# Sparse attention into a softplus MLP on one core: whole-tile loads for the ramp, a V load moved between queues, and two more limits in the kernel's own planner

## The chip, the cores and the metric

The kernel runs on one core of one Trainium2 chip. Its time is the device time of one execution in microseconds (us), and the time of a kernel is the median over several runs. Engines are named as in the profile: PE is TensorE, DVE is VectorE, ACT is ScalarE, POOL is GpSimd, SP is SyncE. A name with a q (SPq, ACTq) is the queue of that engine from which DMAs are issued.

## The reference

Attention over B = 4 batches, H = 8 heads, S = 768 positions, D = 64 with a selection of key chunks, and then an MLP over the 3072 tokens. Cut to what matters:

```python
# attention: chunks of 32 keys, each query keeps the 6 chunks with the highest upper bound
k_min = min over each chunk of k;  k_max = max over each chunk of k
ub = sum over d of maximum(q * k_min, q * k_max)
ub = where(causal by chunk, ub, -1e9)
sel = the top 6 chunks of ub
scores = where(sel and pos_q >= pos_k, q @ k.T / sqrt(D), -1e9)
attn = softmax(scores) @ v
# MLP: tokens x 512 -> 2048 -> 512
h = x @ w_in
g = maximum(h, 0) + log1p(exp(-abs(h)))      # softplus
out = g @ w_out
```

## The kernel before

The work is cut into 12 blocks: 4 batches times 3 query blocks of 256 positions (QB = 256), each of two token tiles of 128 (NT = 2). Heads are taken in four pairs (NP = 4). For each block the kernel loads K, Q and V; brings K and Q into transposed form; reduces K to the minimum and maximum of each chunk (`kx`); forms positive and negative parts of Q (`qp`, `qn`, line 568); multiplies them with the chunk bounds on PE (`ub`, lines 588 and 589); adds the causal mask (L595), takes the largest eight per head (`max`, L604) and compares every chunk with the sixth (`lt`: a compare at L612 and a cast of one column per head at L615, for each token tile in each half of the heads). The comparison result is the mask `mr`. Transposed, it becomes extra rows of the score operands `qa` and `qb`, so that one score matmul (`s`, L691) adds the mask. Exponentials (L700) follow on ACT, the causal select on the diagonal (`cm`, L706) on POOL, the product with V (`av`, L716) on PE, the normalisation (L725, L737) on DVE. The MLP of a block is `h` (L773), exp and log (L779, L783: softplus as log(1 + exp)), and `y` (L794), then a copy (L799) and a store (L803).

The first three blocks (NRAMP = 3, called the ramp here) are prepared with transposes on PE from float32 (`kT` at L490, `qT` at L549, `mT` at L636), with copies on ACT and DVE. Blocks 3 to 11 are prepared with casts on POOL (L457, L459) and transposing DMAs on SP (L509, L559, L651 for the mask, L753 for the attention output).

No order is written by hand. `build` makes a graph of tasks, each with an engine, an assumed duration, a priority and the buffers that it reads and writes. `Graph.schedule` then plays the graph through in assumed time, engine by engine, and the order in which tasks were started becomes the order of the instructions in each engine's program. Some details matter here:

- A task marked `port=True` (and every POOL task that isn't a DMA) starts only when the other engine of DVE and POOL is not in such a task.
- Each DMA is put into a modelled queue after its issue; `lat` is added when it leaves the queue.
- While a spare PSUM buffer is kept (until WARM = 30 us of assumed time), PE gets a fill wherever it has nothing to do: a matmul on a tile of zeros (L355). The fills stand in the program and run whether or not PE would have had to wait.
- A few tasks have an alternative engine (`alt`): the mask copies `ma`, `mb` (L641), the copy `xe` (L750) and the V casts of the ramp (`vc`, L662) go to whichever engine takes them first.

`ramp_loads` issues the loads of the ramp. Of block 0, K and Q are loaded as four half tiles each, by SP and ACT in turn (L389); its two V tiles go one to SP and one to ACT (L386). For blocks 1 and 2, buffer `t` takes the columns of four heads of both token tiles, with two DMAs of 128 KB for each buffer. `hold_pool` (L415) makes POOL read one loaded tile before it issues the weights (L406 and L409, on POOL's queue); which tile, HOLD says. `hold_sp` (L421) does the same on SP for the loads of block 3 onward. In the program that is built, hardware DMAs (those of SP and ACT) take eight semaphores in turn, so each waits until the eighth before it has landed.

Of the kernel before, what the change touches and what calls it, by code (L numbers as in the profile page):

```python
# [13 lines left out]
ACT = mybir.ActivationFunctionType  # L14
# [19 lines left out]
OHP = -98.5  # L34
# [4 lines left out]
RLEAD = 3  # L39
# [7 lines left out]
HOLD = ("q", 0)  # L47
# [22 lines left out]
class Graph:  # L70
# [39 lines left out]
    def schedule(self):  # L110
# [6 lines left out]
        queues, moved = {}, 0.0  # L117
# [24 lines left out]
        def fits(t, eng):  # L142
            if t.alts[eng][2] and port["POOL" if eng == "DVE" else "DVE"] > now + 1e-9:
                return False
# [34 lines left out]
        while True:  # L179
# [27 lines left out]
            for e in LAT:  # L207
# [44 lines left out]
                if t.dma is None:  # L252
                    t.end = now + t.dur + t.lat
                    done(t, t.end)
                else:
                    post(now + DMA_START, "queue", t)
# [4 lines left out]
def build(nc, tiles):  # L261
# [115 lines left out]

    def ramp_loads(n, base, gate):
        for nm in "kqv":
            for t in range(2):  # L380
                b_ = XF[nm, n, t] = Buf("xf")

                def ld(eng, us, nm=nm, t=t, b_=b_):
                    dst = T(b_).rearrange("s (h d) -> s h d", d=D)
                    if nm == "v":
                        eng().dma_start(out=dst, in_=rows(nm, n, t))  # L386
                    else:
                        for u in us:
                            eng().dma_start(out=dst[:, u * 4:u * 4 + 4], in_=rows(nm, n, u)[:, t * 4:t * 4 + 4])  # L389
                pr = base + "kqv".index(nm) + 0.1 * t  # L390
                if n == 0 and nm != "v":
                    for u, eng in ((0, "SP"), (1, "ACT")):
                        add(eng, 0.6, lambda u=u, ld=ld: ld(lambda: AC if u else SP, [u]), pr, w=[(b_, u)],
                            dma=0.585, lat=0.5, name=f"ld{nm}{n}{t}", after=gate)
                else:
                    eng = "ACT" if n == 0 and t == 1 else "SP"
                    add(eng, 0.6 if nm == "v" else 1.2,
                        lambda eng=eng, ld=ld: ld(lambda: AC if eng == "ACT" else SP, range(NT)), pr,
                        w=[(b_, 0), (b_, 1)], dma=1.17, lat=0.5, name=f"ld{nm}{n}{t}", after=gate)

# [65 lines left out]
    def prep(n):  # L466
# [12 lines left out]
        if ramp:  # L479
            for hh in range(2):  # L480
                xk = XF["k", n, hh]
# [3 lines left out]
                def tr(xk=xk, kT=kT):  # L485
                    xv = T(xk).rearrange("s (t p c) -> s t p c", t=NT, p=2)
                    for p in range(2):
                        for t in range(NT):
                            c0 = (p * NT + t) * 128
                            PE.transpose(T(kT)[:, c0:c0 + 128], xv[:, t, p], T("identf"))  # L490
                add("PE", 0.44, tr, pr + 0.01 * hh, r=[(xk, 0), (xk, 1), "identf"], w=[kT], name=f"kT{n}")
# [437 lines left out]
```

## Time and profile before

| what | value |
|---|---|
| median of 8 runs | 265.6 us (264.99 to 267.08) |
| the profiled execution's own time | 264.99 us |
| its span, first to last instruction | 263.3 us |
| granted TensorE clock | 0.999 |
| PE busy | 255.5 us (97%), 2593 matmuls, 133 of them fills |
| ACT busy | 205.0 us (78%) |
| DVE busy | 146.4 us (56%) |
| POOL busy | 85.2 us (32%) |
| load of a K tile of 256 KB, issue to landing | 3.7 us median |
| transposing DMA of the mask, issue to landing | 3.8 us median |

A row of the groups gives line, engine, operation, output and inputs, count, then busy time and mean duration of one, then the engine's idle time before them and what ended it. A row of the timeline starts with the start and the length in us. A row of the chain of waits has start, length and what it was. Rows of PE overlap, since matmuls are pipelined: four matmuls of L773 start 0.109 us apart, though each row lasts 0.27. For DMAs the trace also has the time of each landing.

### The profile page before, as it was taken

Reading aid. Unit: us, or ns where it says so; the run is one execution under the profiler, and the core shown is the slowest. Engines: PE = TensorE matmul, PEld = TensorE weight load, DVE = VectorE, ACT = ScalarE, POOL = GpSimd, SP = SyncE. Lnnn points to the kernel's source line nnn. Section 1 sums busy time; section 2 is a strip of 40 time slices with the busy share of each in tenths; the row PEclk is TensorE's granted clock in tenths of the full one; section 3 lists DMA queues with packets and bytes.
Section 4 is the critical chain, followed back from the end, with each engine's and each line's share of the span. In section 5 each row is a group of like instructions: output and inputs, shape, how many; then the busy total and the mean of one; then the engine's idle time right before and its main releaser. Section 6 shows DMA issues by size and latency. Waiting matters only on the chain.

```text
span 263.3 us, 6800 instructions
## 1 busy us (share of the span) xinstructions
PE 255.5 (97%) x2593; PEld 192.4 (73%) x2593; DVE 146.4 (56%) x549; ACT 205.0 (78%) x369; POOL 85.2 (32%) x179
## 2 busy tenths in 40 slices
PE   8899999999998999999989999999999999999993
PEld 6789997677685776778668768768678778676751
DVE  7489784228597798559998549068363110210202
ACT  5588999997496968999569987949869789576650
POOL 5037542263254560637256521433211111100000
PEclk9999999999999999999999999999999999999999
DMA  7998999979996997999999955885112111130112
GB/s 183 254 223 154 206 206 204 239 98 260 173 268 100 221 244 169 260 225 241 151 232 197 267 139 131 193 167 82 41 46 78 40 41 42 40 84 0 42 40 80
DMA packets 121029, 39.90 MB, mean 152 GB/s; under 512 B 113668, under 2 KB 117764, under 8 KB 120996
## 3 DMA queue, kind: packets, MB, share of 16 engines
q1 hardware_dynamic: 113396, 33.83, 60.3%
q0 software_dynamic: 4448, 4.85, 10.8%
q10 hardware_dynamic: 3152, 0.79, 1.4%
q8 instruction: 20, 0.33, 0.5%
q14 instruction: 13, 0.11, 0.1%
HBM read 27.26 MB, written 6.29 MB: 127 GB/s over the span
## 4 chain that ended last, share of the span: by engine, by line
PE 80%; DVE 8%; DMA 5%; ACT 4%; issue 1%; ACTq 0%; DVEq 0%
PE ps L773 27%; PE ps L794 27%; PE ps L691 13%; PE ps L716 7%; PE ps L355 4%; DMA w<-in_q_dram 2%; DVE kx L513 2%; ACT pt L700 2%; DMA w<-mr 1%; DVE mr L615 1%; DMA w<-in_k_dram 1%; DVE ub L604 1%; ACT e L779 1%; PE ps L549 1%; PE ps L490 1%
## 5 line engine op out<-in xcount | busy, mean ns | idle before, releaser
L794 PE MATMUL ps<-w_out_sb,g 128*128 128x512 bf16 x384 | 106.6, 379 | 0.0
L773 PE MATMUL ps<-x,w_in_sb 128*128 128x256 bf16 x768 | 106.3, 272 | 0.0
L700 ACT ACTIVATE pt<-ps 128x512 bf16<-128x512 f32 (+1 forms) x192 | 93.5, 581 | 5.6 <-PE ps L691 5.3
L773 PEld LDWEIGHTS <-w_in_sb 128*128 128x128 bf16 x768 | 72.9, 98 | 24.8
L779 ACT ACTIVATE e<-ps 128x512 f32<-128x512 f32 x96 | 57.8, 628 | 35.2 <-PE ps L773 34.8
L706 POOL TENSOR_SCALAR_AFFINE_SELECT pt<-pt 128x256 bf16<-128x256 bf16 x96 | 41.0, 432 | 110.9 <-ACT pt L700 110.2
L783 ACT ACTIVATE g<-e 128x1024 bf16<-128x1024 f32 x48 | 51.8, 1080 | 0.9
L794 PEld LDWEIGHTS <-g 128*128 128x128 bf16 x384 | 35.0, 98 | 13.9 <-ACT g L783 0.4
L799 DVE COPY yo<-ps 128x512 f32<-128x512 f32 x24 | 16.4, 685 | 47.8 <-PE ps L794 47.8
L725 DVE RECIPROCAL st<-ps 128x4 f32<-128x4 f32 x48 | 8.6, 182 | 42.3 <-PE ps L716 32.8
L691 PE MATMUL ps<-qab,kb 128*128 128x256 bf16 x192 | 30.5, 259 | 0.2 <-ACT pt L700 0.2
L716 PEld LDWEIGHTS <-pt 128*128 128x128 bf16 x672 | 26.6, 97 | 4.3
L691 PE MATMUL ps<-qab,ka 96*128 96x256 bf16 x192 | 28.9, 259 | 0.9 <-DVE qab L654 0.9
L716 PE MATMUL ps<-v,pt 128*128 128x65 bf16 x672 | 28.5, 193 | 0.0
L459 POOL CAST w<-w 128x512 bf16<-128x512 f32 x36 | 22.0, 629 | 11.0 <-DMA w<-in_k_dram 10.1
L691 PEld LDWEIGHTS <-ka 96*128 96x128 bf16 x192 | 17.8, 97 | 8.5 <-issue 1.2
L513 DVE TENSOR_REDUCE kx<-w 128x32 bf16<-128x1024 bf16 x18 | 21.4, 1209 | 3.3 <-DMA w<-w 3.2
L355 PE MATMUL ps<-zero 128*128 128x256 bf16 x133 | 20.3, 297 | 1.1 <-DVE zero L325 1.1
L691 PEld LDWEIGHTS <-kb 128*128 128x128 bf16 x192 | 16.4, 97 | 6.1 <-issue 0.5
L355 PEld LDWEIGHTS <-zero 128*128 128x128 bf16 x133 | 13.7, 106 | 3.4 <-DVE zero L325 1.1
L737 DVE TENSOR_TENSOR w<-ps,st 128x256 bf16<-128x256 f32 x36 | 15.1, 421 | 1.1
L457 POOL CAST v<-w 128x512 bf16<-128x512 f32 x18 | 11.0, 622 | 12.2 <-DMA w<-in_v_dram 12.2
(64 smaller groups left out, 181.4 us busy)
## 6 DMA issues: line engine op xcount, KB each, us to landing
out_dram<-yo SPq DMA_DIRECT2D x24, 256.0 KB, 2.9
w<-in_v_dram SPq DMA_DIRECT2D x23, 256.0 KB, 3.8
w<-in_k_dram SPq DMA_DIRECT2D x18, 256.0 KB, 3.7
w<-in_q_dram SPq DMA_DIRECT2D x18, 256.0 KB, 4.2
w_in_sb<-in_moe_w_in_dram POOLq DMA_DIRECT2D x4, 512.0 KB, 8.7
w_out_sb<-in_moe_w_out_dram POOLq DMA_DIRECT2D x4, 512.0 KB, 15.1
w<-in_k_dram SPq DMA_DIRECT2D x10, 128.0 KB, 4.5
w<-in_q_dram SPq DMA_DIRECT2D x10, 128.0 KB, 3.8
```

The costliest lines, as they stand in the source:

```text
L355: PE.matmul(T(Fill)[:, 0:256], T("zero")[:, 0:128], T("zero"), start=True, stop=True)
L459: PO.tensor_copy(T(b_)[:, :, t], T(xf).rearrange("s (p c) -> s p c", p=NP))
L513: DV.tensor_reduce(T(kx)[:, m].rearrange("d p (t c) -> d p t c", t=NT), T(kt).rearrange("d (p t) (c s) -> d p t c s", t=NT, s=CH), axis=AX ...
L691: PE.matmul(T(sp)[:, z * QB:z * QB + QB - q0], kk[r0:r1, p, (j + z) * 128:(j + z + 1) * 128], qq[r0:r1, p, q0:QB], start=True, stop=True)
L700: AC.activation(T(pt)[:, j:j + 2].rearrange("k j c -> k (j c)")[:, 0:w], T(sp)[:, 0:w], ACT.Exp, scale=SCALE)
L706: PO.affine_select(out=diag, in_=diag, compare_op=ALU.is_ge, fill=0.0, base=0, channel_multiplier=-1, pattern=[[0, 2], [1, 128]])
L716: PE.matmul(o[:, u, h], T(pts[h])[:, j, c0:c0 + 128], T("v", i)[:, j, 2 * p + h, :], start=(j == 0), stop=(j == t0 + u))
L773: PE.matmul(o, T("w_in")[:, dt, ft * 128:(ft + 1) * 128], T(x)[:, dt], start=(dt == 0), stop=(dt == KDM - 1))
L779: AC.activation(T(e)[:, f2 * 2:f2 * 2 + 2].rearrange("f a s -> f (a s)"), T(hp), ACT.Exp)
L783: AC.activation(T(gb)[:, f4 * 4:(f4 + 1) * 4], T(e), ACT.Ln, bias=1.0)
L794: PE.matmul(T(y), T(gb)[:, f, u * 128:(u + 1) * 128], T("w_out")[:, f, :], start=(f == 0), stop=(f == KFF - 1))
L799: add("DVE", 0.6, lambda y=y, yo=yo: DV.tensor_copy(T(yo), T(y)), pr, r=[y], w=[yo], name=f"yo{n}")
```

## The change

In words, by the parts of the diff:

- Blocks 1 and 2 load K and Q as whole token tiles, one DMA of 256 KB for each, as V always did. `columns` and `landing` are new helpers: the transposes of the ramp take the columns of a head pair from the right buffer, and for blocks 1 and 2 each transpose group reads both token tiles.
- The second V tile of block 0 is issued from SP, as all V tiles are.
- `fits` refuses a DMA of SP or ACT while the eighth before it has not landed in the planner's time.
- The mask compare `lt` is marked as a user of the port that DVE and POOL share.
- Transposing DMAs get a landing latency of TLAT = 1.4 instead of 0.8.
- The constants: RLEAD from 3 to 1 (how far the preparation of a ramp block is put ahead of its attention), OHP from -98.5 to -96 (priority of the two ACT copies at L349), HOLD from `("q", 0)` to `("k", 0)` (the tile of block 2 that POOL waits for before the weights).

The planner places everything anew, so the order of the later blocks changes as well. The new program has 129 fills instead of 133 and the same other matmuls. SP issues 18 DMAs for the ramp instead of 25; ACT loses one DMA issue. One `ma` and one `mb` go from ACT to DVE, one `xe` from DVE to ACT; of the V casts of the ramp, ACT has one of block 0 and one of block 2 (before: one of block 0, one of block 1), POOL the other four.

```diff
 NEG = -30000.0 / SCALE
 BIG = 1.0e30
 NRAMP = 3
-OHP = -98.5
+OHP = -96.0
 W2 = 18
 WARM = 30.0
 COLD = 4.2
 TD = 1.9
-RLEAD = 3
+TLAT = 1.4
+RLEAD = 1
 OPRIO = 25.0
 LEAD = 22
 BG = 40
...
 MSTART = 14.0
 AHEAD = 1.16
 ORDER = "b0 b1 b2 i0 i1 i2 i3 o0 o1 o2 o3".split()
-HOLD = ("q", 0)
+HOLD = ("k", 0)
 
 
 LAT = {"PE": 0.23, "ACT": 0.20, "DVE": 0.15, "POOL": 0.15, "SP": 0.0}
...
         waiting = {e: [] for e in LAT}
         ready = {e: [] for e in LAT}
         events, seq, order = [], 0, []
-        queues, moved = {}, 0.0
+        queues, moved, flying = {}, 0.0, []
 
         def post(at, what, x):
             nonlocal seq
...
         port = {"DVE": 0.0, "POOL": 0.0}
 
         def fits(t, eng):
+            if t.dma is not None and eng != "POOL" and len(flying) >= 8 and (flying[-8].end is None or flying[-8].end > now):
+                return False
             if t.alts[eng][2] and port["POOL" if eng == "DVE" else "DVE"] > now + 1e-9:
                 return False
             for b in t.bufs:
...
                     t.end = now + t.dur + t.lat
                     done(t, t.end)
                 else:
+                    if e != "POOL":
+                        flying.append(t)
                     post(now + DMA_START, "queue", t)
         assert len(order) == len(self.tasks) + len(self.fills), (len(order), len(self.tasks))
         return order
...
     XF, KQ = {}, {}
     landed = {}
 
+
     def ramp_loads(n, base, gate):
         for nm in "kqv":
             for t in range(2):
                 b_ = XF[nm, n, t] = Buf("xf")
-
-                def ld(eng, us, nm=nm, t=t, b_=b_):
-                    dst = T(b_).rearrange("s (h d) -> s h d", d=D)
-                    if nm == "v":
-                        eng().dma_start(out=dst, in_=rows(nm, n, t))
-                    else:
-                        for u in us:
-                            eng().dma_start(out=dst[:, u * 4:u * 4 + 4], in_=rows(nm, n, u)[:, t * 4:t * 4 + 4])
                 pr = base + "kqv".index(nm) + 0.1 * t
                 if n == 0 and nm != "v":
                     for u, eng in ((0, "SP"), (1, "ACT")):
-                        add(eng, 0.6, lambda u=u, ld=ld: ld(lambda: AC if u else SP, [u]), pr, w=[(b_, u)],
-                            dma=0.585, lat=0.5, name=f"ld{nm}{n}{t}", after=gate)
+                        def ld(nm=nm, t=t, b_=b_, u=u, q_=AC if u else SP):
+                            dst = T(b_).rearrange("s (t h d) -> s t h d", t=NT, d=D)
+                            q_.dma_start(out=dst[:, u], in_=rows(nm, n, u)[:, t * 4:t * 4 + 4])
+                        add(eng, 0.6, ld, pr, w=[(b_, u)], dma=0.585, lat=0.5, name=f"ld{nm}{n}{t}", after=gate)
                 else:
-                    eng = "ACT" if n == 0 and t == 1 else "SP"
-                    add(eng, 0.6 if nm == "v" else 1.2,
-                        lambda eng=eng, ld=ld: ld(lambda: AC if eng == "ACT" else SP, range(NT)), pr,
+                    add("SP", 0.6, lambda nm=nm, t=t, b_=b_: SP.dma_start(
+                        out=T(b_).rearrange("s (h d) -> s h d", d=D), in_=rows(nm, n, t)), pr,
                         w=[(b_, 0), (b_, 1)], dma=1.17, lat=0.5, name=f"ld{nm}{n}{t}", after=gate)
+
+
+    def columns(nm, n, hh, p, t):
+        if n == 0:
+            return T(XF[nm, n, hh]).rearrange("s (t p c) -> s t p c", t=NT, p=2)[:, t, p]
+        return T(XF[nm, n, t]).rearrange("s (p c) -> s p c", p=NP)[:, hh * 2 + p]
+
+    def landing(nm, n, hh):
+        return [(XF[nm, n, t], u) for t in ([hh] if n == 0 else range(NT)) for u in range(2)]
 
 
     def weight(nm, c4, pr, after):
...
         js = [blk * NT + t for t in range(NT)]
         if ramp:
             for hh in range(2):
-                xk = XF["k", n, hh]
                 kT = ps("t")
                 p2 = slice(hh * 2, hh * 2 + 2)
 
-                def tr(xk=xk, kT=kT):
-                    xv = T(xk).rearrange("s (t p c) -> s t p c", t=NT, p=2)
+                def tr(hh=hh, kT=kT):
                     for p in range(2):
                         for t in range(NT):
                             c0 = (p * NT + t) * 128
-                            PE.transpose(T(kT)[:, c0:c0 + 128], xv[:, t, p], T("identf"))
-                add("PE", 0.44, tr, pr + 0.01 * hh, r=[(xk, 0), (xk, 1), "identf"], w=[kT], name=f"kT{n}")
+                            PE.transpose(T(kT)[:, c0:c0 + 128], columns("k", n, hh, p, t), T("identf"))
+                add("PE", 0.44, tr, pr + 0.01 * hh, r=landing("k", n, hh) + ["identf"], w=[kT], name=f"kT{n}")
 
                 def kab(which, rs, kT=kT, p2=p2):
                     AC.copy(T(which, i)[rs, p2, ks_], T(kT)[rs].rearrange("d (p s) -> d p s", p=2))
...
 
             def tr(ks=ks, kt=kt):
                 SP.dma_start_transpose(T(kt), T(ks).rearrange("s p t c -> s (p t c)"))
-            add("SP", TD, tr, pr, at=pr - 4, r=[(ks, 0), (ks, 1)], w=[kt], dma=1.15, lat=0.8, name=f"kTd{n}")
+            add("SP", TD, tr, pr, at=pr - 4, r=[(ks, 0), (ks, 1)], w=[kt], dma=1.15, lat=TLAT, name=f"kTd{n}")
             for m in range(2):
                 def red(m=m, kt=kt):
                     DV.tensor_reduce(T(kx)[:, m].rearrange("d p (t c) -> d p t c", t=NT),
...
         c0 = sel[0] * 128
         if ramp:
             for hh in range(2):
-                xq = XF["q", n, hh]
                 qT = ps("t")
                 p2 = slice(hh * 2, hh * 2 + 2)
 
-                def tr(xq=xq, qT=qT):
-                    xv = T(xq).rearrange("s (t p c) -> s t p c", t=NT, p=2)
+                def tr(hh=hh, qT=qT):
                     for p in range(2):
                         for t in range(NT):
                             c0 = (p * NT + t) * 128
-                            PE.transpose(T(qT)[:, c0:c0 + 128], xv[:, t, p], T("identf"))
-                add("PE", 0.44, tr, pr + 0.5 + 0.01 * hh, r=[(xq, 0), (xq, 1), "identf"], w=[qT], name=f"qT{n}")
+                            PE.transpose(T(qT)[:, c0:c0 + 128], columns("q", n, hh, p, t), T("identf"))
+                add("PE", 0.44, tr, pr + 0.5 + 0.01 * hh, r=landing("q", n, hh) + ["identf"], w=[qT], name=f"qT{n}")
 
                 def qe(qT=qT, p2=p2):
                     AC.copy(T(qb)[:, p2], T(qT).rearrange("d (p s) -> d p s", p=2))
...
                 SP.dma_start_transpose(T(qb).rearrange("d p (t s) -> d (p t) s", t=NT),
                                        T(qs).rearrange("s p t c -> s (p t c)"))
             add("SP", TD, tr, pr + 0.5, at=pr - 3, r=[(qs, 0), (qs, 1)],
-                w=[(qb, hh, z) for hh in range(2) for z in range(3)], dma=1.15, lat=0.8, name=f"qTd{n}")
+                w=[(qb, hh, z) for hh in range(2) for z in range(3)], dma=1.15, lat=TLAT, name=f"qTd{n}")
         for hs in ([[0], [1]] if ramp else [[0, 1]]):
             sl = slice(hs[0] * 2, hs[-1] * 2 + 2)
             k_ = len(hs) * (1 if blk else 0.5)
...
                     DV.tensor_copy(m[:, :, :, NCH:NCH + 1], u[:, :, :, NCH:NCH + 1])
             add("DVE", ns * (0.2 + 0.00105 * ne * ncc), lt, pr + 2.3,
                 r=[(ub_sb, hh) for hh in hs] + [(ub_sb, hh, "m") for hh in hs] + [("mr0", 0), ("mr0", 1)],
-                w=[(mr, hh) for hh in hs], name=f"lt{n}")
+                w=[(mr, hh) for hh in hs], port=True, name=f"lt{n}")
         if blk == 0 and ramp:
             add("DVE", 0.15, lambda: DV.memset(T(qa)[64:96, :, 0:128], 0.0), pr + 0.4,
                 w=[(qa, hh, 1) for hh in range(2)], name=f"m0{n}")
...
             def tr(mt=mt):
                 SP.dma_start_transpose(T(mt).rearrange("d p (t s) -> d (p t) s", t=NT),
                                        T(mr).rearrange("s p t c -> s (p t c)"))
-            add("SP", TD, tr, pr + 3, r=[(mr, z) for z in range(3)], w=[mt], dma=1.15, lat=0.8, name=f"mTd{n}")
+            add("SP", TD, tr, pr + 3, r=[(mr, z) for z in range(3)], w=[mt], dma=1.15, lat=TLAT, name=f"mTd{n}")
             add("DVE", 0.36, lambda: DV.tensor_copy(T(qa)[64:96], T(mt)[64:96]), pr + 3,
                 r=[mt], w=[(qa, hh, z) for hh in range(2) for z in (1, 2)], port=True, name=f"ma{n}")
             add("DVE", 0.36, lambda: DV.tensor_copy(T(qb)[32:64], T(mt)[32:64]), pr + 3,
...
         elif p == NP - 1:
             add("SP", TD, lambda: SP.dma_start_transpose(
                 T(x).rearrange("d p (t s) -> d (p t) s", t=NT), T(osb).rearrange("s p t h d -> s (p t h d)")), pr + 1.5,
-                r=[(osb, p_) for p_ in range(NP)], w=[(x, p_) for p_ in range(NP)], dma=1.15, lat=0.8, name=f"oTd{n}")
+                r=[(osb, p_) for p_ in range(NP)], w=[(x, p_) for p_ in range(NP)], dma=1.15, lat=TLAT, name=f"oTd{n}")
 
 
     G = {}
```

## The prediction

> **What bounds the kernel now.** I read the busy shares first, then the groups, the timeline of the first 32 us engine by engine, the chain of waits, and last every place where TensorE's row carries an idle time.
>
> ```profile
> PE 255.5 (97%) x2593; PEld 192.4 (73%) x2593; DVE 146.4 (56%) x549; ACT 205.0 (78%) x369; POOL 85.2 (32%) x179
> ...
> L355 PE MATMUL ps<-zero 128*128 128x256 bf16 x133 | 20.3, 297 | 1.1 <-DVE zero L325 1.1
> ```
>
> TensorE bounds it: it is busy 97% of the span. But 133 of its matmuls are fills on a tile of zeros (second line). They stand in the program at fixed places, so they are not skipped when data comes early. Useful and fill matmuls form one fixed string; the end moves only with the stalls in that string and with its length. The string starts at 1.13 us and its last matmul ends at 259.1; the last copy, store and drain take the other 4.2 us of the 263.3 us span. The profiled execution took 264.99 us, 0.6 below the median of 265.6, so I work out a difference and take it from the median.
>
> The first stall is in the ramp, in the order of time:
>
> ```profile
> 4.91 1.04 ACT L349 COPY kb<-ohb 32x1024 bf16<-32x1024 bf16 x1
> ...
> 9.02 0.38 ACTq L386 DMA_DIRECT2D w<-in_v_dram  x1
> ...
> 9.50 0.58 ACT L494 CAST ka<-ps 64x512 bf16<-64x512 f32 x1 [3.55 <-DVE kx L497]
> ...
> 10.71 0.58 ACT L553 CAST qab<-ps 128x512 bf16<-128x512 f32 x1
> ...
> 11.32 0.36 DVE L568 TENSOR_SCALAR qpn<-qab 128x256 bf16<-128x256 bf16 x2 [1.58 <-ACT qab L553]
> ...
> 11.61 0.18 PE L588 MATMUL ps<-bd,qpn 128*128 128x16 bf16 x1 [0.97 <-DVE qpn L568]
> ```
>
> ScalarE stands still for 3.55 us before its first cast of K. The profile blames VectorE's reduction (L497), but that one had ended at 6.38. What ended last is the V load on ScalarE's own queue at 9.02: the chain has "DMA w<-in_q_dram" just before it, landed at 9.00. In the program each hardware DMA waits for the eighth before it, and this is the one that held ScalarE. Behind it wait the casts of K, then of Q (10.71), then VectorE's qpn (11.32), then the first bound matmul (L588, 0.97 idle).
>
> The second kind of stall comes in the middle. Four views of the same stretch follow: VectorE's timeline, GpSimd's, the chain of waits, TensorE's timeline.
>
> ```profile
> 78.17 0.59 DVE L615 CAST mr<-ub 128x4 bf16<-128x4 f32 x1
> ...
> 80.17 0.58 DVE L615 CAST mr<-ub 128x4 bf16<-128x4 f32 x1
> ...
> 78.12 1.23 POOL L459 CAST w<-w 128x512 bf16<-128x512 f32 x2
> ...
> 80.05 1.22 POOL L459 CAST w<-w 128x512 bf16<-128x512 f32 x2
> ...
> 80.77 3.83 DMA w<-mr
> ...
> 85.10 0.54 PE L691 MATMUL ps<-qab,ka 96*128 96x256 bf16 x4 [0.67 <-DVE qab L654]
> ...
> 132.32 0.20 PE L588 MATMUL ps<-bd,qpn 128*128 128x48 bf16 x1 [0.38 <-DVE qpn L568]
> ...
> 133.39 0.54 PE L691 MATMUL ps<-qab,ka 96*128 96x256 bf16 x4 [0.19 <-DVE qab L654]
> ```
>
> A cast of four columns (L615) takes 0.58 while GpSimd casts, against 0.16 when GpSimd is idle. The mask of block 4 is late by it, its transpose takes 3.83 us from issue, and TensorE waits at 85.10. Rows of matmuls overlap by about 0.16 us, so a shown idle of 0.67 is a stall of some 0.83.
>
> **The change part by part.**
>
> *V of block 0 off ScalarE.* The issue (0.38 us) goes to SP, right behind the other V tile. ScalarE's order is then ohb casts, K casts, Q cast, with nothing between. The K casts start when L497 is done, at 6.4, and end at 7.6. The Q cast waits for its transposes, which end at 9.22 in the trace (8.62 + 0.60), and ends at 9.8 instead of 11.29. Then qpn ends at 10.2, but TensorE must first pass the second Q transposes (9.93, four at 0.11) and one fill, so the bound matmul starts at about 10.5 instead of 11.61. Second half: K casts from 9.9 to 11.05, Q cast to 11.65 (before 12.96), qpn to 12.03. TensorE, with 14 fills at 0.109 (the row "11.83 1.58 ... x13", less 0.16, divided by 13), arrives at 12.13. Before, the second bound matmul stood at 13.29. The next link, the mask transpose at 13.84, keeps its 0.5 us after qpn: 12.55. Saved: 1.1 to 1.3, with the small lags of those links 1.45; I take **1.45**. The price: V tile 1 is now ahead of K of block 1 on SP. Its own eighth DMA before is a half tile of K that landed at 4.24, so it is issued at about 4.25; it lands near 10.3, where the first 256 KB of K landed before (10.26). ScalarE casts it at 11.65, so 1.3 us of cover.
>
> *Whole tiles for blocks 1 and 2.* 16 half-tile issues become 8; SP's ramp list goes from 25 DMAs to 18. From 9.00 to 16.45 the landings of the trace give 7.5 tiles of 256 KB, 0.99 us each; later SP's issues limit them and the last lands at 23.1. Thirteen tiles at 0.99 from 9.0 end at 21.9, in order: K of block 1 complete at 12.0, Q at 13.9, first K tile of block 2 at 16.9. Both halves of a transpose group now need both tiles, so the first half of K waits for 12.0 instead of 10.26. TensorE reaches those transposes at 15.58 − 1.45 + 5 more fills (0.55) + two matmuls, about 14.8: cover of 2.8 us, and without it each late us stops TensorE for one. I cost it at **0**, between −0.5 (an earlier consumer) and +0.5.
>
> *Another gate for the weights.* GpSimd now looks at K of block 2 instead of Q, and does so after the eight selects of block 0 and two V casts. Six exponentials follow each other on ScalarE from about 13.75 (15.19 − 1.45); with a K cast (1.17), two more exponentials, a select (0.41) and two casts (0.61 each) the gate opens near 20.0, against 22.25. The trace has 6.0 us from the first weight issue to its landing (22.38 to 28.40), so it lands at 26.0 to 26.2. In the new order the first projection matmul (L773) has 129 fills and 126 other matmuls ahead of it, before 133 and 142: 30.01 − 1.45 − 0.44 − 1.5 (eight Q transposes at 0.11, four mask transposes at 0.06, four score matmuls at about 0.1, all moved behind) = 26.6. So the weights cover by about 0.5. Between 0 and +1; I take **+0.2**.
>
> *Planner's priorities (RLEAD, OHP), the eight-in-flight test, the longer landing of transposes.* They cost no instruction. They only order. The four fills fewer are worth 0.44 where nothing waits; block 2's masks come later in the order and their copies on ScalarE stand close ahead of their score matmuls. In the trace ScalarE is busy 9.00 of 9.00 us from 31 to 40, so I set the 0.44 against a wait there: **0**.
>
> *Mask compares on the shared port.* In the kernel's own plan the compares of blocks 2 to 11 lay 5.7 us over GpSimd's work; in the new plan none does. Of the 40 casts at L615, 20 overlap GpSimd in the trace (median 0.40) and 20 don't (0.165). The Trainium skill, "SBUF — State Buffer", section "Who interferes with whom", speaks partly against it: the pair of ports is an exclusive lock held for a whole instruction, so the wait isn't removed but changes hands; a compare held back for GpSimd is late too. By the rule alone I would take 0. By the rows, block 4's two compare groups took 1.39 and 1.12 us against 0.53 planned, 1.45 too much on the path, of which 0.83 reached TensorE; blocks 7 and 8 lost 0.54, 0.29 and 0.31. That is 1.97. The plan only avoids overlaps if the two engines keep step, and in the trace their lags differ by 0.2 to 1 us. I take a bit under half, **0.95**, between 0 and 1.97. A gain here can also be undone: a compare that waits delays a transpose on SP, and behind it queue the loads of the next block.
>
> Sum: −1.45 − 0.95 + 0.2 = −2.2, and 265.6 − 2.2 = **263.4**.
>
> **The rivals.**
>
> *Front only.* The ramp gains 1.45, the mask waits return elsewhere because a new order makes new tight places. Against it: compares cleared of GpSimd. For it: TensorE already waits for four different producers. −1.2 + 0.2: 264.6.
>
> *Weights gate the start.* If the weight transfers share the DMA engines with the last loads (until 21.9) and land at 28.4 as before, the first projection matmul waits 1.8 us with no fill to use: −2.2 − 0.2 + 1.8 gives 265.0. Against it: data flowed only some 3.5 us after the issue in the trace.
>
> *Slower: V of block 2 on ScalarE.* One of its two V casts is now in ScalarE's order, between exponentials, at about 37 us; before, both were GpSimd's. If the weights (512 KB each 2.55 us) starve that last load, ScalarE stops, and everything behind it, and TensorE within a us or two. It decides once the tile lands later than 37; 2.2 + 0.8 us later, at 40, the kernel is slower, and at 41 it takes 267.2. Against it: the tile should land near 21, before the weights flow.
>
> *All of it.* Every mask stall goes: −1.45 − 1.97 = 262.2.
>
> **How the numbers follow.** 0.3% is 0.8 us, about what a measurement of this kernel can tell from no change. Likeliest case (ramp and part of the masks) 0.52, all of it 0.11, front only 0.17, weights 0.08, slower by V or by another wait of the new order 0.12. Faster: 0.52 + 0.11 + 0.13 of front only = 0.76; same 0.04 + 0.08 = 0.12; slower 0.12. The range leaves out most of the slower case: 261.7 to 265.8; the likeliest case alone spans 262.4 to 264.3.
>
> **What would show it.** ScalarE's idle before its first K cast falls from 3.55 to about 0.4; the first bound matmul starts near 10.5 and the first projection near 26.6; the casts at L615 have a mean under 0.25 instead of 0.288; the idle at the first scores of blocks 4 and 7 shrinks. I am wrong if TensorE's first projection comes after 28, if ScalarE shows a wait for a V load after 30 us, or if block 3 onward shows idle on TensorE above 2.5 us in sum.

## The result and the profile after

| | before | after | ratio, 95% interval |
|---|---|---|---|
| median, first comparison | 265.65 us | 263.24 us (12 runs) | 0.9904 [0.9883, 0.9925] |
| median, second comparison | 266.57 us | 263.96 us (6 runs) | 0.9911 [0.9881, 0.9940] |
| profiled execution, its own time | 264.99 us | 261.71 us | |
| its span | 263.3 us | 260.0 us | |

The change makes the kernel about 0.9% faster: 2.4 us by the medians of the first comparison, where 2.2 was predicted. The ratios leave out the few runs in a slow state (one of the 12 of the changed kernel, 267.29 us), so they differ a little from the quotients of the medians. The profiled execution of the changed kernel is 1.5 us below its own median, and a part of what it shows is luck. That part has to be found first.

The page of the changed kernel, busy shares and the row of the fills:

```profile
PE 252.8 (97%) x2589; PEld 191.0 (73%) x2589; DVE 148.5 (57%) x550; ACT 203.6 (78%) x368; POOL 83.9 (32%) x179
...
L360 PE MATMUL ps<-zero 128*128 128x256 bf16 x129 | 18.1, 286 | 1.1 <-DVE zero L330 1.1
```

TensorE is still the bound, with four fills fewer. The ramp, in the timeline of the changed kernel:

```profile
6.47 0.58 ACT L500 CAST ka<-ps 64x512 bf16<-64x512 f32 x1 [0.53 <-DVE kx L503]
...
7.89 0.58 ACT L557 CAST qab<-ps 128x512 bf16<-128x512 f32 x1 [0.23 <-PE ps L553]
...
8.52 0.36 DVE L572 TENSOR_SCALAR qpn<-qab 128x256 bf16<-128x256 bf16 x2
...
9.11 0.17 PE L592 MATMUL ps<-bd,qpn 128*128 128x16 bf16 x1
```

ScalarE's idle before its first cast of K is 0.53 instead of 3.55, and what ends it now is really VectorE's reduction. The first bound matmul no longer waits and starts at 9.11 instead of 11.61. But 2.5 us is more than the V load had cost. The rest is in TensorE's timeline, in a group of 16 fills that is the same in both programs. First the kernel before, then the changed one:

```profile
4.73 2.86 PE L355 MATMUL ps<-zero 128*128 128x256 bf16 x16
```

```profile
4.30 1.91 PE L360 MATMUL ps<-zero 128*128 128x256 bf16 x16
```

The same fills took 2.86 us in one execution and 1.91 in the other. In both traces the fills start 0.213 us apart at first and 0.109 apart later, so TensorE runs at half its pace until some moment. Before the change that moment comes at about 6.6 us, after it at 3.9. I call this the clock coming up; the granted clock of the profile reads 1.00 in both, microsecond by microsecond from 0 to 9, and doesn't show it. Up to this point nothing in the change touches TensorE's program.

To sort such effects I compare each group of matmuls with its due time in the program's own plan. Between stalls TensorE runs nearly at the pace of the plan, so a step up in the lag (actual start less due time) is a stall. Worked out from the two traces and plans:

| lag of TensorE in us, at | before | after |
|---|---|---|
| first K transposes (first load) | 0.69 | 0.68 |
| second K transposes (clock) | 1.50 | 0.13 |
| second mask transposes of block 0 (V load) | 3.00 | 0.13 |
| ahead of the first scores of block 4 | 3.49 | 0.69 |
| behind them | 4.38 | 1.80 |
| last matmul | 5.04 | 1.73 |

The last matmul is due at 253.48 in the plan of before and at 253.47 in that of after. The 3.3 us between the spans are therefore lag alone: 1.37 from the clock, 1.50 from the V load, and 0.44 from everything behind the ramp.

That 0.44 is a balance. The waits of blocks 7 and 8 before (0.55, 0.28 and 0.31) shrink to 0.17 or are gone; others are new (0.59 ahead of the bound matmuls of block 3, 0.54 at the scores of block 6). Block 4 is worse than before, 1.04 instead of 0.83. Four views of that place, VectorE's and GpSimd's timelines, the chain of waits and TensorE's timeline of the changed kernel:

```profile
77.33 0.18 DVE L729 RECIPROCAL st<-ps 128x4 f32<-128x4 f32 x1 [0.36 <-ACT e L783]
...
78.18 0.58 DVE L619 CAST mr<-ub 128x4 bf16<-128x4 f32 x1
...
78.80 0.58 DVE L619 CAST mr<-ub 128x4 bf16<-128x4 f32 x1
...
78.06 1.85 POOL L467 CAST w<-w 128x512 bf16<-128x512 f32 x3
...
79.41 4.23 DMA w<-mr
...
84.13 0.54 PE L695 MATMUL ps<-qab,ka 96*128 96x256 bf16 x4 [0.87 <-DVE qab L658]
```

The plan had put these casts clear of GpSimd. On the chip a reciprocal ahead of them waited for 0.36 us (its row names ScalarE, the chain of waits has TensorE's `av` of 77.04 just before it), GpSimd did not wait with it, and two of VectorE's casts met its three casts after all: 0.58 each instead of 0.17.

### The profile page after: what moved, and what is told of

Its sections match the earlier page's. It is cut to its first block, busy times and chain, and to the rows that moved or that the text cites. A ratio compares the mean times of both kernels' runs of the same rounds, so it can differ in the third digit from the quotient of the medians.

```text
span 260.0 us, 6786 instructions
## 1 busy us (share of the span) xinstructions
PE 252.8 (97%) x2589; PEld 191.0 (73%) x2589; DVE 148.5 (57%) x550; ACT 203.6 (78%) x368; POOL 83.9 (32%) x179
## 4 chain that ended last, share of the span: by engine, by line
PE 86%; DVE 5%; ACT 4%; DMA 2%; issue 1%; DVEq 0%
PE ps L798 29%; PE ps L777 28%; PE ps L695 13%; PE ps L720 7%; PE ps L360 5%; DVE kx L519 2%; DMA w<-mr 2%; ACT g L787 1%; ACT pt L704 1%; DVE qpn L572 1%; PE ps L496 1%; PE ps L593 1%; ACT e L783 1%; PE ps L592 1%; DVE bd L536 1%
## 5 line engine op out<-in xcount | busy, mean ns | idle before, releaser
L798 PE MATMUL ps<-w_out_sb,g 128*128 128x512 bf16 x384 | 105.3, 379 | 0.0
L710 POOL TENSOR_SCALAR_AFFINE_SELECT pt<-pt 128x256 bf16<-128x256 bf16 x96 | 39.3, 413 | 119.1 <-ACT pt L704 118.0
L467 POOL CAST w<-w 128x512 bf16<-128x512 f32 x36 | 21.9, 623 | 8.7 <-DMA w<-in_k_dram 7.9
L519 DVE TENSOR_REDUCE kx<-w 128x32 bf16<-128x1024 bf16 x18 | 21.3, 1211 | 2.7 <-DMA w<-w 2.7
L360 PE MATMUL ps<-zero 128*128 128x256 bf16 x129 | 18.1, 286 | 1.1 <-DVE zero L330 1.1
L360 PEld LDWEIGHTS <-zero 128*128 128x128 bf16 x129 | 12.6, 102 | 2.9 <-DVE zero L330 1.1
L608 DVE MAX8 ub<-ub 128x8 f32<-128x24 f32 (+2 forms) x160 | 14.3, 161 | 0.2
```

What stands on the lines that cost most here:

```text
L360: PE.matmul(T(Fill)[:, 0:256], T("zero")[:, 0:128], T("zero"), start=True, stop=True)
L467: PO.tensor_copy(T(b_)[:, :, t], T(xf).rearrange("s (p c) -> s p c", p=NP))
L519: DV.tensor_reduce(T(kx)[:, m].rearrange("d p (t c) -> d p t c", t=NT), T(kt).rearrange("d (p t) (c s) -> d p t c s", t=NT, s=CH), axis=AX ...
L710: PO.affine_select(out=diag, in_=diag, compare_op=ALU.is_ge, fill=0.0, base=0, channel_multiplier=-1, pattern=[[0, 2], [1, 128]])
L798: PE.matmul(T(y), T(gb)[:, f, u * 128:(u + 1) * 128], T("w_out")[:, f, :], start=(f == 0), stop=(f == KFF - 1))
```

## The experiments

"After" is the changed kernel, and every ratio is against the kernel before on the same chip.

**The second V tile of block 0 from SP, nothing else.** The order that the planner wrote before is kept; only the queue of this one DMA differs.

```diff
-                        lambda eng=eng, ld=ld: ld(lambda: AC if eng == "ACT" else SP, range(NT)), pr,
+                        lambda ld=ld: ld(lambda: SP, range(NT)), pr,
```

> The kernel before, with its planner untouched, except that the second V tile of block 0 is issued from SP at the same place of the program instead of from ScalarE. Theory (a wait for the eighth DMA before holds ScalarE): ScalarE's idle of 3.55 us before its first K cast falls under 1, the first bound matmul comes 1.1 to 1.4 us earlier, the time falls by 1.1 to 1.5 us (ratio 0.994 to 0.996). Rival (the ramp gains by whole-tile loads, V is a bystander): no change, ratio 1.000.

Measured: 264.14 us, ratio 0.9931 [0.9906, 0.9956], or 1.8 us (1.2 to 2.5 by the interval). ScalarE's timeline of this kernel:

```profile
6.47 0.58 ACT L494 CAST ka<-ps 64x512 bf16<-64x512 f32 x1 [0.27 <-DVE kx L497]
```

The idle of 3.55 is gone, and with it the stall at the bound matmuls. By the ratios this single queue brings most of what the whole change brings, though the intervals overlap. A new wait takes some of it back in this profile: the first weights land at 28.15, and the first projection stands 0.83 us for them by the lag.

**The new order, with that V tile back on ScalarE.**

```diff
-                    add("SP", 0.6, lambda nm=nm, t=t, b_=b_: SP.dma_start(
+                    add("SP", 0.6, lambda nm=nm, t=t, b_=b_: (AC if (n, nm, t) == (0, "v", 1) else SP).dma_start(
```

> The changed kernel with its order kept, except that the second V tile of block 0 is issued from ScalarE again, now right after the two copies of the chunk rows, where its eighth DMA before is a half tile of Q that lands near 6.1 us. Theory (what cost time was the late landing that the issue waited for, not the queue): ScalarE issues it by 6.5, its K cast starts within 0.3 us of the changed kernel's, and the time equals the changed kernel's within 0.4 us (ratio to the kernel before about 0.991). Rival (any DMA on ScalarE's queue in the ramp costs): 1 us or more is lost, ratio about 0.995.

Measured: 262.94 us, ratio 0.9906 [0.9879, 0.9932], the same as after. ScalarE's timeline of this kernel:

```profile
6.55 0.38 ACTq L396 DMA_DIRECT2D w<-in_v_dram  x1
7.03 0.58 ACT L500 CAST ka<-ps 64x512 bf16<-64x512 f32 x1 [1.06 <-PE ps L496]
```

The queue as such is not what cost time. The issue goes out at 6.55, not 9.02, although it is on the same engine, since with whole tiles and the new order the eighth DMA before it is another one. In the trace of before the issue waits for the semaphore of ScalarE's own half tile of Q, which lands at 9.00; here it waits for that of SP's half tile of Q, which lands at 6.53. What had cost time was the landing that the issue had to wait for. The cast of K does start 0.56 us later than in the profile of after, where at most 0.3 was expected, since the issue now stands ahead of it; the median shows no loss by that.

**The same from the other side: the kernel before with whole tiles only.** V stays on ScalarE; the planner, without its new limit and constants, gives 137 fills.

```diff
-                        for u in us:
-                            eng().dma_start(out=dst[:, u * 4:u * 4 + 4], in_=rows(nm, n, u)[:, t * 4:t * 4 + 4])
...
+                    add(eng, 0.6, lambda nm=nm, t=t, b_=b_, eng=eng: (AC if eng == "ACT" else SP).dma_start(
+                        out=T(b_).rearrange("s (h d) -> s h d", d=D), in_=rows(nm, n, t)), pr,
...
-                add("PE", 0.44, tr, pr + 0.01 * hh, r=[(xk, 0), (xk, 1), "identf"], w=[kT], name=f"kT{n}")
+                add("PE", 0.44, tr, pr + 0.01 * hh, r=landing("k", n, hh) + ["identf"], w=[kT], name=f"kT{n}")
```

> The kernel before with the whole-tile loads of blocks 1 and 2 alone; V of block 0 stays on ScalarE, constants and planner as before (137 fills). Theory (loads are not what holds the ramp; the V issue is): ScalarE still stands for about 3 us before its first K cast, time within 0.8 us of the kernel before, ratio 0.998 to 1.003. Rival (fewer and larger DMAs carry the gain): 1 us or more faster, 0.996 or less.

Measured: 266.72 us, ratio 1.0038 [1.0011, 1.0066], slower. Its ScalarE timeline:

```profile
6.30 0.39 ACTq L391 DMA_DIRECT2D w<-in_v_dram  x1
6.80 0.58 ACT L495 CAST ka<-ps 64x512 bf16<-64x512 f32 x1 [0.67 <-DVE kx L498]
```

The expectation missed: ScalarE was to stand for about 3 us, but the stall of the ramp is gone here as well, with V still on ScalarE, because the issue again waits for the half tile of Q of SP (landed at 6.28). Yet the kernel is slower: the new order adds four fills and stalls of its own later (1.01 us at the scores of block 7, 0.56 at those of block 2, 0.50 at the first output matmuls, by the lag), and this plan is 1.3 us longer. One repaired wait of 1.5 us can be lost to the order that the planner writes for it.

**The threshold column by a reduction instead of a cast, in the changed kernel and in the kernel before.** If the cast of four columns is what suffers from GpSimd, an operation that does not suffer takes the wait away without any plan.

```diff
-                    DV.tensor_copy(m[:, :, :, NCH:NCH + 1], u[:, :, :, NCH:NCH + 1])
+                    DV.tensor_reduce(m[:, :, :, NCH:NCH + 1], u[:, :, :, NCH:NCH + 1], axis=AX.X, op=ALU.max)
```

> The changed kernel with its order kept; the 40 casts of one threshold column are written as a reduction over a single element, which computes the same. Theory (the mask is late because this cast waits for GpSimd's use of the shared port; reductions in this trace have one duration beside GpSimd or not): no instance above 0.25 us, TensorE's stall before the scores of block 4 shrinks from 1.0 to under 0.5, time 0.5 to 1.0 us below the changed kernel, ratio to the kernel before about 0.988. Rival (the mask is late for its transpose or the chain ahead of it): same time as the changed kernel, 0.991.

> The kernel before with its order kept and the same reduction in place of the 40 casts. Theory: the stall before the scores of block 4 (0.83) goes, and those of blocks 7 and 8 (0.54, 0.29, 0.31) in part; time falls by 1.0 to 1.9 us, ratio 0.993 to 0.996. Rival (mask lateness has another cause): ratio 1.000.

Measured in the changed kernel: 263.41 us, ratio 0.9912 [0.9883, 0.9942], no gain over after, where 0.5 to 1.0 us was expected. In the kernel before: 265.01 us, ratio 0.9964 [0.9937, 0.9991], about 0.9 us, a little under the 1.0 to 1.9 expected. Block 4's masks in VectorE's timeline of the changed kernel with the reduction:

```profile
79.53 0.37 DVE L616 TENSOR_TENSOR mr<-ub 128x64 bf16<-128x64 f32 x1
79.82 0.16 DVE L619 TENSOR_REDUCE mr<-ub 128x4 bf16<-128x4 f32 x1
79.89 0.57 DVE L616 TENSOR_TENSOR mr<-ub 128x64 bf16<-128x64 f32 x1
```

The reduction takes 0.16 even beside GpSimd, and the compare ahead of it now takes 0.37 and 0.57 instead of 0.22. The wait moved one instruction on. The groups say it for the whole kernel, first after, then after with the reduction:

```profile
L619 DVE CAST mr<-ub 128x4 bf16<-128x4 f32 x40 | 10.9, 273 | 0.0
L616 DVE TENSOR_TENSOR mr<-ub 128x64 bf16<-128x64 f32 (+2 forms) x40 | 9.3, 235 | 0.1
```

```profile
L616 DVE TENSOR_TENSOR mr<-ub 128x64 bf16<-128x64 f32 (+2 forms) x40 | 11.4, 291 | 0.1
L619 DVE TENSOR_REDUCE mr<-ub 128x4 bf16<-128x4 f32 x40 | 6.5, 162 | 0.0
```

Of the 4.4 us saved at L619, L616 takes 2.1 back. Whether that is the whole reason why no time was gained is open: the stall at block 4 is still 0.71 us by the lag, and in this execution the first projection waited 1.59 us for the weights (see below), which can hide a gain of some tenths.

**The mark for the shared port, alone in the kernel before, and taken out of the changed one.**

```diff
-                w=[(mr, hh) for hh in hs], name=f"lt{n}")
+                w=[(mr, hh) for hh in hs], port=True, name=f"lt{n}")
```

> The kernel before with the mask compares marked as users of the shared port, nothing else. The prediction's step: 0.95 us faster, ratio 0.9965. Theory after the trace: within 0.5 us of the kernel before, 0.998 to 1.002, with the casts at the threshold column still near 0.5 us where GpSimd works.

> The changed kernel with the mask compares not marked as users of the shared port; the planner places all anew (129 fills as well). The prediction's step (marking saves 0.95 us): slower than the changed kernel by about 0.9, ratio to the kernel before 0.994. Theory after the trace (on the chip the compares of the tight blocks still meet GpSimd, since the engines don't keep the planner's step): within 0.5 us of the changed kernel, 0.990 to 0.993.

Measured: alone, 265.52 us, ratio 0.9989 [0.9966, 1.0012], nothing clear. Taken out of the changed kernel, 264.19 us, ratio 0.9930 [0.9906, 0.9954], 0.0026 above after or about 0.7 us, with intervals that overlap. Without the mark, block 4 in VectorE's, GpSimd's and TensorE's timelines:

```profile
79.91 0.43 DVE L616 TENSOR_TENSOR mr<-ub 128x64 bf16<-128x64 f32 x1
80.27 0.59 DVE L619 CAST mr<-ub 128x4 bf16<-128x4 f32 x1
...
80.22 1.17 POOL L467 CAST w<-w 128x512 bf16<-128x512 f32 x2
...
85.87 0.54 PE L695 MATMUL ps<-qab,ka 96*128 96x256 bf16 x4 [1.41 <-DVE qab L658]
```

The stall at block 4 is 1.57 us by the lag, against 1.04 in the profile of after. Over the whole kernel the compares and casts do not get shorter by the mark: lines 616 and 619 take 19.5 us in sum without it and 20.3 with it. And the plan without the mark is itself 0.20 us longer. So what the mark is worth in the changed kernel, and by which way, isn't settled by this pair. In the alone-run the two lines do shrink, from 21.3 to 19.2 us, and behind the ramp the lag grows by 1.09 us up to the last matmul (before: 2.04), but the order that comes with the mark takes this back: its plan is 0.55 us longer, and in that execution the V load cost 3.8 us of lag in the ramp (before: 1.5).

**The weights.** In the changed kernel the first projection waited in most profiles. TensorE's timeline, of the run with V back on ScalarE and of the run with the reduction:

```profile
26.75 0.61 PE L777 MATMUL ps<-x,w_in_sb 128*128 128x256 bf16 x4 [0.61 <-DMA w_in_sb<-in_moe_w_in_dram]
```

```profile
27.70 0.61 PE L777 MATMUL ps<-x,w_in_sb 128*128 128x256 bf16 x4 [1.42 <-DMA w_in_sb<-in_moe_w_in_dram]
```

By the lag, the five profiles in which GpSimd issues the weights where after does show stalls of 0 (after), 0.29 (after, second profile), 0.36, 0.77 and 1.59 us. To take this wait away, the first quarter of the weights is issued after the sixth select of block 0, before GpSimd's last two selects, the V casts and the look at K:

```diff
     order = graph.schedule()
+    first = next(t for t in order if t.name == "ldw_in")
+    order.remove(first)
+    sixth = [i for i, t in enumerate(order) if t.name == "cm0"][5]
+    order.insert(sixth + 1, first)
```

> The changed kernel with its order kept, except that GpSimd issues the first quarter of w_in after the sixth causal select of block 0 (about 3 us earlier, in a stretch where GpSimd waits). Theory (since the V stall is gone, the landing of the first weights sets the first projection matmul in most executions): no idle on TensorE before the first projection, its start at 25 to 26.6 us, time 0.3 to 1.0 us below the changed kernel's 263.2, ratio to the kernel before 0.987 to 0.990. Rival (the weights' wait was an accident of two profiles): no change, 0.991. Loss if the 512 KB push back the loads of block 2: up to +1 us.

Measured: 262.24 us, ratio 0.9867 [0.9841, 0.9893], with no wait at the first projection. It was run again, together with after:

> The changed kernel with the first quarter of the expert's input weights issued after the sixth select of the cumulative maximum, a second time. If the weights' landing costs the changed kernel on average about 1 us, this stands at 0.986 to 0.988 of the kernel before, some 1 us under the changed kernel on the same chip, and its first projection waits for nothing. If the first result was chance, it stands with the changed kernel at 0.990 to 0.992.

> The changed kernel once more, beside the kernel with its first quarter of the weights issued two GpSimd selects later to earlier (w1_again), on one chip. If the weights' landing is what the changed kernel still loses in most of its executions, it comes to 0.990 to 0.992 of the kernel before, and its profile shows either a wait at the first projection of 0.3 to 1.6 us or, where the clock warmed late, none. If the difference between the two seen so far (0.4 %) was chance, both stand at the same ratio.

Measured: 264.10 us, ratio 0.9887 [0.9846, 0.9927], and after 263.96 us, ratio 0.9911 [0.9881, 0.9940]. The second time the gain is not clear, and the runs fall into two groups: of the twelve, five lie between 261.45 and 262.92, five between 264.93 and 265.22. The profile is of one of the long ones. Its GpSimd timeline, its chain of waits and its TensorE timeline:

```profile
16.15 0.77 POOL L414 DMA_DIRECT2D w_in_sb<-in_moe_w_in_dram  x1
...
15.63 7.61 DMA w<-in_k_dram
...
23.28 0.55 PE L496 MATMUL ps<-identf,w 128*128 128x128 f32 x3 [1.73 <-DMA w<-in_k_dram]
```

The second K tile of block 2 was issued at 15.63, half a microsecond ahead of the weight, and landed at 23.24, after 7.6 us, just behind the weight (23.07). In the first profile of the same kernel that tile had been issued near 14.2, 2.2 us ahead of the weight (16.42), it had landed at 18.77, and the weight caught the loads behind them, for which nobody waited. So an early weight can catch a load that is on the path, and it then stops TensorE for 2 us. By these two profiles, what decides is how far the K tile on SP's queue is ahead of the weight on GpSimd's, which differs from one execution to the next. That the other four long runs have the same cause is likely and not shown.

From this follows a place in between: late enough for the last K tile to be well under way, early enough for the first projection. The same edit, with the eighth select instead of the sixth:

```diff
-    sixth = [i for i, t in enumerate(order) if t.name == "cm0"][5]
-    order.insert(sixth + 1, first)
+    eighth = [i for i, t in enumerate(order) if t.name == "cm0"][7]
+    order.insert(eighth + 1, first)
```

> The first quarter of the expert's input weights issued after the eighth select of block 0, near 18.1 us, instead of after the sixth (16.2 to 16.4) or behind the two V casts (18.7 to 20.1). If a weight that starts before the last K tile of block 2 has landed delays that tile by 5 us and TensorE by 2 us, and a weight that starts too late keeps the first projection waiting by 0.3 to 1.6 us, this place escapes both: every execution lies between 261 and 264, the ratio at 0.985 to 0.989, and the profile shows no wait above 0.3 us at the second K transposes of block 2 or at the first projection. If the delay of loads isn't tied to the place of the weight, executions near 265 appear as they did with the weight after the sixth select.

Measured: 262.17 us, ratio 0.9855 [0.9812, 0.9898], four runs between 261.36 and 262.39 and none near 265. The weight lands at 25.50 in its trace; TensorE, which comes at 25.61, does not wait, though by a margin of 0.1 us only. Four runs are few: the first six with the weight after the sixth select had none near 265 either. GpSimd's and TensorE's timelines:

```profile
17.52 0.77 POOL L414 DMA_DIRECT2D w_in_sb<-in_moe_w_in_dram  x1
...
25.61 0.60 PE L777 MATMUL ps<-x,w_in_sb 128*128 128x256 bf16 x4
```

The last V tile of block 2 pays for the early weight: it lands at 34.59 in this trace, against 24.81 in the first profile of after. GpSimd casts it at 36.3, so here nobody waits.

**The value matmuls of block 8.** The second profile of after has a stall that the first had not. GpSimd's timeline, the chain of waits and TensorE's timeline:

```profile
158.60 0.62 POOL L465 CAST v<-w 128x512 bf16<-128x512 f32 x1 [3.03 <-DMA w<-in_v_dram]
159.17 0.41 POOL L710 TENSOR_SCALAR_AFFINE_SELECT pt<-pt 128x256 bf16<-128x256 bf16 x1
...
153.04 5.51 DMA w<-in_v_dram
...
159.63 0.33 PE L720 MATMUL ps<-v,pt 128*128 128x65 bf16 x5 [0.92 <-POOL pt L710]
...
160.57 0.56 PE L720 MATMUL ps<-v,pt 128*128 128x65 bf16 x13 [0.61 <-POOL pt L710]
```

The cast of V of block 10 isn't needed for long, but it stands ahead of selects of block 8 on GpSimd. Its load came late, GpSimd stood 3.03 us, and TensorE lost 1.89 behind the selects. By the lag this stall was 0, 0.26, 0.30, 1.16 and 1.89 in the five profiles with the weights as in after; none of the five profiles that lack the new order (the kernel before and the experiments on it) has a stall at the value matmuls of block 8. With the weight after the eighth select and these two casts moved behind the fifth select of block 8:

```diff
+    late = [t for t in order if t.name == "cv10"]
+    for t in late:
+        order.remove(t)
+    fifth = [i for i, t in enumerate(order) if t.name == "cm8"][4]
+    order[fifth + 1:fifth + 1] = late
```

> The same, and GpSimd's two casts of V of block 10 moved behind the fifth select of block 8, so that those selects no longer stand behind a late V load. In one profile of the changed kernel this held the value matmuls of block 8 up by 1.9 us, in others by 0 to 1.2. If such waits are common, this is 0.3 to 0.8 us faster than the kernel with the weight after the eighth select alone, and its profile shows no wait of the value matmuls of block 8 above 0.3 us. If the late V load was rare, or something else behind it is as late, the two are equal within 0.3 us.

Measured: 261.95 us, ratio 0.9853 [0.9818, 0.9889], level with the kernel without this edit. Their TensorE timelines, first without, then with it:

```profile
158.17 0.57 PE L720 MATMUL ps<-v,pt 128*128 128x65 bf16 x13 [1.07 <-POOL pt L710]
```

```profile
157.84 0.82 PE L720 MATMUL ps<-v,pt 128*128 128x65 bf16 x22
```

The stall of 1.25 us is gone in the profile. That both profiled executions have a span of 260.6 is made up elsewhere: the second K transposes came at 6.08 in the first and at 6.86 in the second, and the second quarter of the weights held TensorE for 0.52 in the second. A gain by this edit is plausible and not shown. These two have the lowest ratios of the case; their intervals still touch that of after.

## Why the prediction was right, and where its steps were off

The median (263.24 against 263.4), the direction and the leading term were right. Step by step:

- *V of block 0 off ScalarE, −1.45.* Right in its mechanism; in size 1.50 by the lag in the first pair of profiles and 1.8 by the ratio of the run that does only this (1.2 to 2.5). What it missed is that the V load also hid something. The landing near 9.0 held ScalarE whether the clock had come up or not. In the run of before with the reduction, the second K transposes came at 6.23 instead of 7.42, and the first bound matmul moved only from 11.61 to 11.20. With the wait gone, an early clock counts in full, and the first bound matmul came at 9.11 where 10.5 was predicted. The profile that the step was read from had a late clock (a lag of 1.50 at the second K transposes; the mean of all 14 profiles is 0.83), so on average the step should bring about 0.7 more than it brought there, an estimate from these lags. The fix named in the step (another queue) was not the only one that works: whole tiles alone removed the stall, and with the new order the tile may stay on ScalarE.
- *Whole tiles, 0.* In the changed kernel the loads came as predicted: the last six landings of the ramp are 17.0, 17.9, 18.8, 19.8, 20.7 and 24.8; 21.9 was predicted for the last, which the weights delayed and which nobody awaited. That the step is worth 0 was not measured by itself: tiles alone made the kernel about 1 us slower, by the order that the planner wrote for them.
- *Another gate for the weights, +0.2.* Too small. The first profile shows the predicted cover (landed 25.03, used at 25.50), the four others with this gate show waits up to 1.59, and the mean of the five is 0.6. The step took 6.0 us from issue to landing, from one row; the fourteen profiles gave 5.4 to 8.4. The bound "between 0 and +1" was too narrow, and the rival that the weights gate the start was real in some executions.
- *Four fills fewer, 0.* Right, since the last matmul is due at the same time in both plans. The wait at block 2's scores that the step set against them is 0.24 by the lag, no more than before (0.33).
- *Mask compares on the shared port, −0.95.* About right in size, not shown in its reason. In the first pair of profiles everything behind the ramp gained only 0.44, but the first profile of after is not typical there. From the first projection to the last matmul, without the waits for V in block 8 and for the second weights, the lag grows by 2.1 us in the profile of before and by 1.6 in that with V from SP. In the seven profiles with the changed order and the cast it grows by 0.6 to 1.3, with a median of 0.7; without the mark by 1.8. The compares and casts themselves hardly changed (21.3 us in sum before, 20.3 after, 19.5 without the mark), so it is open whether the gain comes from keeping them clear of GpSimd or from other places of the new order. The caution taken from the Trainium skill, "SBUF — State Buffer", section "Who interferes with whom" (an exclusive lock, so the wait changes hands) was in place: overlapped casts went from 20 to 16 of 40 only, L619's mean fell from 0.288 to 0.273, not under 0.25, and block 4's stall grew, where the text had it shrink.
- *What no step had.* A late V load that holds GpSimd's selects of block 8, up to 1.9 us in the new order (0.7 in the mean of the five profiles). The slower rival had the right kind (a V cast in the order of an engine that others need) on the wrong engine and at the wrong time: ScalarE never waited for V of block 2 in the profile of after, GpSimd did for V of block 10. Its figure of 267.2 for a landing at 41 is a slip, 267.4 by its own rate; nothing hangs on it. The mark "TensorE idle above 2.5 us from block 3 on" was kept in the first profile (2.3 by the listed steps) and broken in the second (3.5).

That the net lies so near is in part luck: the ramp brought more than predicted, the weights cost more, and the late V load was not in the sum. How the 2.4 us of the medians divide between masks, weights and late V loads isn't settled, since the last two differ from one execution to the next, and each kernel has one or two profiles.

## What to carry to other kernels

When an issue on a compute engine's queue stands still, ask which earlier DMA's landing it has to wait for before the queue is blamed: any change to the number of DMAs ahead moves that wait. In a fixed order, an instruction that nobody needs soon should not stand ahead of one that is needed, if it waits for a load; and a large transfer should start neither so early that it catches a load on the path nor so late that its own user waits. Before a profiled difference is credited to a change, look at a stretch that the change does not touch.

## What was not expected of the hardware

- TensorE's clock. In 14 profiles, whose TensorE programs are alike up to the second K transposes, these came between 6.05 and 7.53 us, while the fills began at about 1.1 in all of them. The last fill at half pace starts at 3.66 in the earliest (after) and at 6.64 in the latest (after, second profile), and the programs with the old loads spread as the others do (6.17 to 7.42). The Trainium skill, "TensorE: Matmul & The Clock Gate", section "Part 1: The HAM clock gate (the "warmup" mystery)", calls the cold start a budget of time, not of matmuls, that varies from run to run because its window is free-running. The traces agree that it varies; the section puts the variation at ±500 ns, and here it is larger, 3 us in the moment and so 1.5 us in what follows. That is over half of what the change brings.
- A 256 KB load that was under way when a 512 KB weight began took 7.6 us, against 3.7 in the median of the K loads before the change, and the weight itself took 5.4 to 8.4 us. Which of two queues' transfers lands first isn't told by which was issued first.
- A cast of four columns takes 0.17 us alone and in most cases 0.4 to 0.6 beside GpSimd, a reduction over the same four columns 0.16 in either case. With the reduction it is the compare (two inputs in SBUF) that is often longer beside GpSimd: at 128x64, 0.37 to 0.57 in six of seven cases, against one of seven in the profile of after.
